# One-core mixer kernel: VectorE instead of GpSimd sums weight quarters; other budgets for side work; two products of a pair change places and banks swap by pairs

## The chip, the cores and the metric

The kernel runs on one core of one Trainium2 chip. The metric is device time in microseconds, median of several runs of the whole program. Before the change it is 978.81 us (three runs, 978.65 to 979.02).

## What is computed

A chain of three blocks over 4 x 576 tokens of 512 features, all in fp32 with every matrix product made of three rounded products (high x high, high x low, low x high):

```python
def reference(q, k, v, omega, moe_*, moe2_*):
    x = random_feature_attention(q, k, v, omega)          # 8 heads of 64, 128 features
    x = x + (relu(x.T @ w_tok1) @ w_tok2).T               # token mixing
    x = x + relu(x @ moe_w_ch1) @ moe_w_ch2               # first channel MLP, 512 -> 1536 -> 512
    u = x + real(fft(fft(x, axis=1), axis=2))             # over tokens, then features
    un = (u - mean(u)) / sqrt(var(u) + 1e-6)
    return u + relu(un @ moe2_w_ch1) @ moe2_w_ch2         # second MLP, 512 -> 2048 -> 512
```

## The kernel before, in words

Weights come in as 64-bit words. `widen` turns each slab on VectorE (seven instructions, L341 to L372) into two fp32 halves and stores them in DRAM tensors `kept`; this and the transform are **side work**.

The stages, in order of time in the profile: attention (to about 204 us), the first MLP in five token blocks (`ch_block`, to about 536 us), the second MLP in two **plain** blocks (`ff_block`, block 0 of 512 tokens to about 651 us, block 1 of 256 tokens to about 704 us), and two **paired** blocks of 768 tokens (`paired_block`, to the end).

One step of `mlp` is: twelve up-products into a bank H (L776), relu on ScalarE (`hh`, L860), `hl` on VectorE (L861), side work, then the twelve down-products of the step before (L898 in the first MLP, L1259 in the second), and in the plain blocks a second helping of side work. TensorE, VectorE and ScalarE each take their instructions strictly in the order in which this Python code emits them.

`Side` hands out side work. `step(budget)` adds to a credit that is capped at SAVED_US and runs items, each with an estimated cost, from a queue `lead` and then from a queue `rest` until the credit is used; `None` in a queue makes it pause for `apart` steps. CH_US, FF_US and S_US are the budgets of a step in the first MLP, the plain blocks and the paired blocks. In `lead` stand the transforms `dft(b)` (the chains even0 to even4 and odd0 to odd3 on VectorE, L957 to L1024 with L978, feeding the TensorE products L1050 to L1061, then L1077 and L1090) and the normalisations `norm(c)` (L1158 to L1186).

`sum_pair(p)` makes, for the paired blocks, four sums and differences of quarters of the weights of a pair of slabs: one 128x1024 addition and four 128x256 ones on GpSimd (L1214 to L1218), a rounding on ScalarE (L1222), a 128x1024 difference on GpSimd (L1226), and a store by SyncE's queue (L421). It runs for pairs 0 to 6 during block 0 and for pair 7 in block 1. GpSimd has no other arithmetic after attention, only DMA issues.

In `paired_block` each pair of slabs takes seven products by Strassen-like sums, six matmuls each (`product`, L1455), into two banks X and Y, with the down-products of the pair before in between (`run`, L1468):

```python
X = P1;   s1 = X;          Y = P6;  u2 = Y + s1       # L1497, L1499
X += P2;  relu of X;       Y = P5;  vv = Y + u2       # L1461, L1507
Y += P3;  held0 = Y + u2;  X = P7;  held1 = X + vv    # L1513, L1515
X += P4;  c21 = X + u2;    relu of c21                # L1521, L1461
```

After each of the four parts comes a step of side work (`pace`). In paired block 0 that is the last transform and `norm(3)`. The operands of P3 lie in `buh`, those of P7 in `bul`; for paired block 0 they are made at its start by `prepare_late`.

Of the kernel before, what the change touches and what calls it, by code (L numbers as in the profile page):

```python
# [14 lines left out]
ALU = mybir.AluOpType  # L15
# [5 lines left out]
B, H, S, D, M = 4, 8, 576, 64, 128  # L21
# [11 lines left out]

SLOT0_US, SLOT1_US, SLOT_US, FIRST_US, SHORT_US, CH_US, FF_US, S_US, SAVED_US = 1.2, 0.45, 1.2, 3.9, 1.2, 4.0, 3.0, 1.5, 4.0


NP = NFF // 2
HALF = 384  # L40
# [3 lines left out]
ROWS = PLAIN + PAIRED  # L44
P1, P2, P4, P6, P3, P7, P5 = 0, 1, 3, 4, 5, 6, 7
# [156 lines left out]
class Side:  # L202
# [5 lines left out]
    def __init__(self):  # L208
        self.lead, self.rest, self.issues = [], [], []
        self.credit = 0.0  # L210
        self.steps = 0
        self.apart, self.waited = 1, 0
        self.defer = DEFER

    def later(self, fn, steps=None):
# [9 lines left out]
    def step(self, budget):  # L225
        self.steps += 1
        while self.issues and self.issues[0][0] <= self.steps:
            self.flush()
        self.credit = min(self.credit + budget, SAVED_US)
        for queue in (self.lead, self.rest):  # L230
            while queue:
                if queue[0] is None:
                    self.waited += 1
                    if self.waited >= self.apart:
                        queue.pop(0)
                        self.waited = 0
                    break
                if queue[0][0] > self.credit:
                    return
                item = queue.pop(0)  # L240
                self.credit -= item[0]
                item[1]()
# [60 lines left out]
def mix_kernel(ctx: ExitStack, tc: tile.TileContext, qt, kt, va, om, w1, w2, wch, wff, t1, t2, out):  # L303
# [97 lines left out]
    whole = set()  # L401
# [44 lines left out]
    def bank(tag):  # L446
        if tag not in pools:
            tag = "A"
        if tag == "A" and spare:

            tag = spare.pop(0)
            spare.append(tag)
        pl, bufs = pools[tag]
        return pl.tile([128, 512], F32, tag=tag, name=tag, bufs=bufs)
# [251 lines left out]
    side = Side()  # L706
# [22 lines left out]
    def turns(n, c):  # L729
        return list(range(n)) if c % 2 == 0 else list(range(n))[::-1]  # L730
# [176 lines left out]
    u = mlp0["u"]  # L907
# [6 lines left out]
    u = u2  # L914
# [278 lines left out]
    def ff_split(c, u, kks):  # L1193
        n = 128 * len(ROWS[c])
        for kk in kks:
            pb = bank("S")
            for t in range(len(ROWS[c])):
                pe.transpose(pb[:, t * 128:t * 128 + 128], uns[c, t][:, kk * 128:kk * 128 + 128], ident)
            act.copy(out=u[0][:, kk, 0:n], in_=pb[:, 0:n])
            dve.tensor_tensor(out=u[1][:, kk, 0:n], in0=pb[:, 0:n], in1=u[0][:, kk, 0:n], op=ALU.subtract)  # L1200

    def ff_prepare(c, u):
        return [lambda: (side.until(lambda: (c, len(ROWS[c]) - 1) in uns, side.lead), ff_split(c, u, (0, 1))),
                lambda: ff_split(c, u, (2, 3))]

    def sum_pair(p):

        k = p % 2  # L1210
        w = mix.get((1, p))
        y = cv.tile([128, 1024], F32, tag=f"cvy{k}", name="cvy")
        v = y.rearrange("p (c n) -> p c n", c=4)
        pool.tensor_tensor(out=v, in0=w[:, :, 0], in1=w[:, :, 1], op=ALU.add)  # L1214
        pool.tensor_tensor(out=v[:, 3], in0=v[:, 2], in1=v[:, 3], op=ALU.add)
        pool.tensor_tensor(out=v[:, 2], in0=v[:, 0], in1=v[:, 2], op=ALU.subtract)
        pool.tensor_tensor(out=v[:, 0], in0=v[:, 3], in1=v[:, 0], op=ALU.subtract)
        pool.tensor_tensor(out=v[:, 1], in0=v[:, 1], in1=v[:, 0], op=ALU.subtract)  # L1218
        so = cv.tile([128, 2, 1024], F32R, tag=f"cvo{k}", name="so")

        def high():
            act.copy(out=so[:, 0], in_=y)  # L1222
            side.later(low, 1)

        def low():
            pool.tensor_tensor(out=so[:, 1], in0=y, in1=so[:, 0], op=ALU.subtract)  # L1226
            side.later(store, 3)

        def store():
            keep(sync, kept[1, p][:, 4:8], so)  # L1230
            whole.add((3, p))

        side.later(high, 4)

    def put_out(r, acc):
        x = row(r)
# [144 lines left out]
    for at_ in range(1, NBLK):  # L1381

        if at_ == 3:
            leave_slots()
            f2 = ctx.enter_context(tc.tile_pool(name="f2", bufs=1, side="right", reuse_waits="tile"))
            l3 = ctx.enter_context(tc.tile_pool(name="l3", bufs=2, side="right", reuse_waits="tile"))
        if at_ == 4:
            side.lead += norm(0)
        if at_ in (3, 4):
            side.lead += dft(at_ - 3)  # L1390
        v = operand()
        last = at_ + 1 == NBLK
        ch_block(at_, BLOCKS[at_], u, ff_prepare(0, v) if last else [lambda: ch_split(BLOCKS[at_ + 1], v)],
                 SHORT_US if at_ == 1 else CH_US)
        u = v

    side.apart = 2
    side.lead += norm(1) + dft(2)
    v = operand()
    ff_block(0, u, ff_prepare(1, v), FF_US)()  # L1400
    side.lead += norm(2) + [None, (0.0, begin_ff)] + prepare_early(0) + prepare_early(1)
# [81 lines left out]
    def paired_block(c, todo, uses, after):  # L1483
# [6 lines left out]
                side.step(S_US)  # L1490

        for p_ in range(NP):
            X, Y = (bank("H")[:, 0:HALF] for _ in range(2))
            h = hbuf[4 * (p_ % 2):4 * (p_ % 2) + 4]
            w = ffw.get((1, p_, 0))
            product(X, w[:, 0], P1, True)
            act.copy(out=s1, in_=X)  # L1497
            product(Y, w[:, 1], P6, True)
            dve.tensor_tensor(out=u2, in0=Y, in1=s1, op=ALU.add)  # L1499
            ffw.used()  # L1500
            pace()
            run(todo, 4)
            w = ffw.get((1, p_, 1))
            product(X, w[:, 0], P2, False)
            relu_parts(h[0:2], X)
            product(Y, w[:, 1], P5, True)
            dve.tensor_tensor(out=vv, in0=Y, in1=u2, op=ALU.add)  # L1507
            pace()
            run(todo, 5)
            ffw.used(1 + uses)  # L1510
            w = ffw.get((1, p_, 2))
            product(Y, w[:, 0], P3, False)
            dve.tensor_tensor(out=held[p_][:, 0], in0=Y, in1=u2, op=ALU.add)  # L1513
            product(X, w[:, 1], P7, True)
            dve.tensor_tensor(out=held[p_][:, 1], in0=X, in1=vv, op=ALU.add)  # L1515
            ffw.used()
            pace()
            run(todo, 4)
            w = ffw.get((1, p_, 3))
            product(X, w[:, 0], P4, False)  # L1520
            dve.tensor_tensor(out=c21, in0=X, in1=u2, op=ALU.add)  # L1521
            relu_parts(h[2:4], c21)
            pace()
            run(todo)
            ffw.used(1 + uses)
            if after:
                after()
            after, uses = None, 1
            if p_ == 0:
                acc = [bank("A") for _ in range(RT)]  # L1530
            for s_ in range(2):
                todo += downs(acc, h[2 * s_:2 * s_ + 2], (2, p_, s_), p_ + s_ == 0, p_ + s_ == NP)
# [62 lines left out]
```

## Time and profile before

| | |
|---|---|
| median of three runs | 978.81 us |
| the profiled execution's own time | 980.43 us |
| its span (first to last instruction) | 978.70 us |
| TensorE busy / VectorE busy / GpSimd busy | 943.6 / 631.0 / 180.7 us |
| mean granted TensorE clock | 0.989 of full speed |

In the profile PE is TensorE's matmuls, PEld its weight loads, DVE VectorE, ACT ScalarE, POOL GpSimd, SPq SyncE's queue. A row of the timeline has the start, the duration of the group of like instructions that begins there, the engine, line, operation, tile written and read, shape, count, and in brackets the idle time just before and what ended it. Matmuls are pipelined and their ends modelled, so distances of starts are the safer measure of TensorE's progress.

### The profile page before, as it was taken

The page shows a single profiled execution, that of the slowest core. Times are in us where ns is not written, and L with a number is a line of the kernel's source. Part 1 is how long each engine was busy: PE and PEld are TensorE (multiplying, and loading weights), DVE is VectorE, ACT ScalarE, POOL GpSimd, SP SyncE. Part 2 cuts the span into 40 slices and gives each one's busy share as a digit, 9 for nine tenths or more (in the row PEclk, how much of TensorE's full clock was granted, in tenths as well). Part 3 has the DMA queues.
Part 4 walks back from the last instruction along what each step waited for, and adds up shares of the span by engine and source line. Part 5 has one row for each costly group of instructions (what it writes and reads, how often), then busy time and mean ns, then how long its engine had stood idle before and what let it go on. Part 6 is the DMA issues. An engine that isn't in the chain of part 4 may idle for free.

```text
span 978.7 us, 14096 instructions
## 1 busy us (share of the span) xinstructions
PE 943.6 (96%) x5362; PEld 835.8 (85%) x5362; DVE 631.0 (64%) x1222; ACT 301.1 (31%) x676; POOL 180.7 (18%) x158
## 2 busy tenths in 40 slices
PE   7999998999999999999999996899999999999998
PEld 7999897988889888888888885788888998899986
DVE  5997989886775777767765366446475466543342
ACT  5976666642212322122211111122221113311121
POOL 3443333321210122000004063640000000000000
PEclk9999999999999999999999997999999999999999
DMA  7764454388898576562446374538756666677764
GB/s 265 234 202 171 146 218 154 139 307 322 314 408 331 188 273 228 203 248 108 172 173 224 120 235 152 172 119 331 290 195 206 219 209 213 221 263 256 249 209 162
DMA packets 68258, 216.48 MB, mean 221 GB/s; under 512 B 5600, under 2 KB 14432, under 8 KB 54240
## 3 DMA queue, kind: packets, MB, share of 16 engines
q1 hardware_dynamic: 60992, 172.40, 50.6%
q0 software_dynamic: 7056, 43.06, 12.0%
q8 instruction: 42, 0.69, 0.3%
q14 instruction: 24, 0.20, 0.1%
q10 hardware_dynamic: 144, 0.13, 0.0%
HBM read 169.30 MB, written 42.47 MB: 216 GB/s over the span
## 4 chain that ended last, share of the span: by engine, by line
PE 83%; DVE 13%; ACT 2%; issue 1%; DMA 0%; DVEq 0%; ACTq 0%
PE H L776 21%; PE A L898 15%; PE A L1468 13%; PE H L1455 11%; PE A L1259 6%; PE A L506 3%; PE N L582 2%; PE A L667 2%; PE H L540 2%; DVE mx L520 1%; PE S L1077 1%; DVE cvo L364 1%; PE S L1090 1%; PE S L680 1%; PE A L565 1%
## 5 line engine op out<-in xcount | busy, mean ns | idle before, releaser
L776 PE MATMUL H<-uh,w 128*128 128x512 f32 (+1 forms) x736 | 214.9, 360 | 1.5 <-ACT x L621 1.5
L776 PEld LDWEIGHTS H<-uh,w 128*128 128x128 f32 x736 | 133.5, 190 | 22.1 <-ACT x L621 1.7
L860 ACT ACTIVATE hh<-H 128x512 fp32r<-128x512 f32 (+1 forms) x92 | 49.1, 533 | 298.2 <-PE H L776 298.1
L776 PE MATMUL H<-ul,w 128*128 128x512 f32 (+1 forms) x368 | 132.0, 359 | 0.0
L861 DVE SCALAR_TENSOR_TENSOR hl<-H,hh 128x512 fp32r<-128x512 f32 (+1 forms) x92 | 56.0, 608 | 107.9 <-ACT hh L860 107.6
L898 PE MATMUL A<-hh,w 128*128 128x512 f32 (+1 forms) x480 | 108.7, 369 | 0.0
L1468 PE MATMUL A<-w2t,b 128*128 128x512 f32 x384 | 100.8, 394 | 0.0
L898 PEld LDWEIGHTS A<-hh,w 128*128 128x128 f32 x480 | 84.2, 188 | 15.0
L1455 PE MATMUL H<-b,w1t 128*128 128x384 f32 x480 | 92.0, 337 | 1.7 <-DVE t L1515 0.9
L1455 PEld LDWEIGHTS H<-b,w1t 128*128 128x128 f32 x480 | 83.9, 188 | 7.3 <-DVE t L1515 3.4
L1468 PEld LDWEIGHTS A<-w2t,b 128*128 128x128 f32 x384 | 70.6, 188 | 11.6
L776 PEld LDWEIGHTS H<-ul,w 128*128 128x128 f32 x368 | 69.8, 190 | 10.0
L524 ACT ACTIVATE f<-A,mx 128x128 f32<-128x128 f32 x200 | 57.6, 393 | 27.6 <-DVE mx L520 23.5
L898 PE MATMUL A<-hl,w 128*128 128x512 f32 (+1 forms) x240 | 59.2, 368 | 0.0
L1259 PE MATMUL A<-w,hh 128*128 128x512 f32 x192 | 52.5, 406 | 0.0
L520 DVE TENSOR_REDUCE mx<-A 128x4 f32<-128x512 f32 x71 | 48.1, 681 | 3.1 <-PE A L506 2.1
L898 PEld LDWEIGHTS A<-hl,w 128*128 128x128 f32 x240 | 42.6, 188 | 7.6
L364 DVE SCALAR_TENSOR_TENSOR cvo<-cvo,stg 128x1024 f32<-128x1024 int32 (+2 forms) x32 | 41.1, 1283 | 0.0
L540 PE MATMUL H<-v,f 128*128 128x65 f32 x320 | 40.1, 270 | 0.9 <-ACT f L524 0.9
L1259 PEld LDWEIGHTS A<-w,hh 128*128 128x128 f32 x192 | 35.3, 194 | 6.2
L540 PEld LDWEIGHTS H<-v,f 128*128 128x128 f32 x320 | 38.9, 191 | 1.3 <-ACT f L524 1.1
L360 DVE SCALAR_TENSOR_TENSOR cvo<-cvy,cvo 128x1024 int32<-128x1024 int32 (+2 forms) x32 | 38.6, 1207 | 0.5
(254 smaller groups left out, 1728.6 us busy)
## 6 DMA issues: line engine op xcount, KB each, us to landing
w<-kept SPq DMA_DIRECT2D x60, 1024.0 KB, 6.7
w2t<-kept SPq DMA_DIRECT2D x55, 512.0 KB, 4.9
w1t<-kept SPq DMA_DIRECT2D x48, 512.0 KB, 4.8
stg<-in_wff_dram POOLq DMA_DIRECT2D x16, 1024.0 KB, 6.3
kept<-cvo POOLq DMA_DIRECT2D x13, 1024.0 KB, 6.2
stg<-in_wch_dram SPq DMA_DIRECT2D x9, 1024.0 KB, 6.0
kept<-cvo POOLq DMA_DIRECT2D x16, 512.0 KB, 7.0
kept<-so SPq DMA_DIRECT2D x16, 512.0 KB, 9.4
```

Of the source, the lines that this page charges most:

```text
L360: dve.scalar_tensor_tensor(out=st["h"], in0=st["y"].bitcast(I32), scalar=-0x80000000, in1=st["h"], op0=ALU.bitwise_and, op1=ALU.bitwise_or)
L364: dve.scalar_tensor_tensor(out=st["l"].bitcast(F32), in0=st["l"], scalar=2.0 ** 32, in1=st["lw"].bitcast(U32), op0=ALU.mult, op1=ALU.add)
L520: dve.tensor_reduce(out=mx, in_=p4, axis=AX.X, op=ALU.max, negate=True)
L524: act.activation(out=f[:, hh], in_=p4[:, hh], func=AF.Exp, bias=mx[:, hh])
L540: pe.matmul(out=kvp[b, g][:, hh * 65:hh * 65 + 65], lhsT=ft["k", i, g][:, hh, :], rhs=src["v", i, int(off > 0)][:, 4 * g + hh, :], start=( ...
L776: pe.matmul(out=hb[:, 0:n], lhsT=w(a, kk), rhs=u[:, kk, 0:n], start=(c == 0), stop=(c == 11))
L860: act.activation(out=hh, in_=hb[:, 0:n], func=AF.Relu)
L861: dve.scalar_tensor_tensor(out=hl, in0=hb[:, 0:n], scalar=0.0, in1=hh, op0=ALU.max, op1=ALU.subtract)
L898: pe.matmul(out=acc[i][:, 0:cols], lhsT=a[:, cs], rhs=v, start=(n == 0 and c_ == 0), stop=(n == NCH - 1 and c_ == 2))
L1259: pe.matmul(out=acc[t], lhsT=a[:, t * 128:t * 128 + 128], rhs=w, start=(n == 0 and c_ == 0), stop=(n == NFF - 1 and c_ == 2))
L1455: pe.matmul(out=to, lhsT=w[:, a, cs], rhs=v[:, q], start=(start and n == 0), stop=(n == 5), skip_group_check=True)
L1468: pe.matmul(out=acc[t], lhsT=h[n // 2][:, t * 128:t * 128 + 128], rhs=w[:, n % 2], start=(begins and n == 0), stop=(ends and n == 2))
```

## The change

- `sum_pair` makes its sums on VectorE instead of GpSimd, in line with the other work of that engine, and earlier after one another: the first addition at once, the other four at the next step, the rounding one step after those, the difference one step later (cost estimates 1.2, 1.5 and 1.2), the store two steps after that.
- Budgets: CH_US 4.0 to 4.3, FF_US 3.0 to 3.8, SAVED_US 4.0 to 4.6.
- `norm(0)` and `norm(1)` go to the queue `rest`, and each queue counts its own pauses.
- In a pair, P7 and its sum come ahead of P3 and its sum, and every second pair takes the two banks in the other order.

```diff
-SLOT0_US, SLOT1_US, SLOT_US, FIRST_US, SHORT_US, CH_US, FF_US, S_US, SAVED_US = 1.2, 0.45, 1.2, 3.9, 1.2, 4.0, 3.0, 1.5, 4.0
+SLOT0_US, SLOT1_US, SLOT_US, FIRST_US, SHORT_US, CH_US, FF_US, S_US, SAVED_US = 1.2, 0.45, 1.2, 3.9, 1.2, 4.3, 3.8, 1.5, 4.6
...
-        for queue in (self.lead, self.rest):
+        for n, queue in enumerate((self.lead, self.rest)):
             while queue:
                 if queue[0] is None:
-                    self.waited += 1
-                    if self.waited >= self.apart:
+                    self.waited[n] += 1
+                    if self.waited[n] >= self.apart:
                         queue.pop(0)
-                        self.waited = 0
+                        self.waited[n] = 0
                     break
...
-        return [lambda: (side.until(lambda: (c, len(ROWS[c]) - 1) in uns, side.lead), ff_split(c, u, (0, 1))),
+        return [lambda: (side.until(lambda: (c, len(ROWS[c]) - 1) in uns, side.rest), ff_split(c, u, (0, 1))),
...
+        side.until(lambda: p not in turns(NP, 0)[2:] or (3, p - 2) in whole, side.lead)
         w = mix.get((1, p))
...
-        pool.tensor_tensor(out=v, in0=w[:, :, 0], in1=w[:, :, 1], op=ALU.add)
-        pool.tensor_tensor(out=v[:, 3], in0=v[:, 2], in1=v[:, 3], op=ALU.add)
-        pool.tensor_tensor(out=v[:, 2], in0=v[:, 0], in1=v[:, 2], op=ALU.subtract)
-        pool.tensor_tensor(out=v[:, 0], in0=v[:, 3], in1=v[:, 0], op=ALU.subtract)
-        pool.tensor_tensor(out=v[:, 1], in0=v[:, 1], in1=v[:, 0], op=ALU.subtract)
         so = cv.tile([128, 2, 1024], F32R, tag=f"cvo{k}", name="so")
+        dve.tensor_tensor(out=v, in0=w[:, :, 0], in1=w[:, :, 1], op=ALU.add)
+        side.credit -= 1.2
+
+        def sums():
+            dve.tensor_tensor(out=v[:, 3], in0=v[:, 2], in1=v[:, 3], op=ALU.add)
+            dve.tensor_tensor(out=v[:, 2], in0=v[:, 0], in1=v[:, 2], op=ALU.subtract)
+            dve.tensor_tensor(out=v[:, 0], in0=v[:, 3], in1=v[:, 0], op=ALU.subtract)
+            dve.tensor_tensor(out=v[:, 1], in0=v[:, 1], in1=v[:, 0], op=ALU.subtract)
+            side.later(high, 1)
 
         def high():
             act.copy(out=so[:, 0], in_=y)
-            side.later(low, 1)
+            side.later(lambda: side.lead.insert(0, (1.2, low)), 1)
 
         def low():
-            pool.tensor_tensor(out=so[:, 1], in0=y, in1=so[:, 0], op=ALU.subtract)
-            side.later(store, 3)
+            dve.tensor_tensor(out=so[:, 1], in0=y, in1=so[:, 0], op=ALU.subtract)
+            side.later(store, 2)
...
-        side.later(high, 4)
+        side.lead.insert(0, (1.5, sums))
...
         if at_ == 4:
-            side.lead += norm(0)
+            side.rest[0:0] = norm(0)
...
-    side.lead += norm(1) + dft(2)
+    side.lead += [(0.0, lambda: side.rest.extend(norm(1)))] + dft(2)
...
-            X, Y = (bank("H")[:, 0:HALF] for _ in range(2))
+            X, Y = [bank("H")[:, 0:HALF] for _ in range(2)][::(1, -1)[p_ % 2]]
...
+            product(X, w[:, 1], P7, True)
+            dve.tensor_tensor(out=held[p_][:, 1], in0=X, in1=vv, op=ALU.add)
             product(Y, w[:, 0], P3, False)
             dve.tensor_tensor(out=held[p_][:, 0], in0=Y, in1=u2, op=ALU.add)
-            product(X, w[:, 1], P7, True)
-            dve.tensor_tensor(out=held[p_][:, 1], in0=X, in1=vv, op=ALU.add)
```

Where the instructions move. The lines of the changed program are higher by 2 from `sum_pair` on and by 5 behind it.

**VectorE in block 0, around the even chain of the third transform.** `cvy` and `so` are the sums, `w` the weights, `fo` and `fv` the transform. Before:

```order
L861 SCALAR_TENSOR_TENSOR hl<-H,hh 128x512
L973 TENSOR_TENSOR fv<-fo 128x289
L974 TENSOR_TENSOR fv<-fo 128x289
L975 COPY fv<-sp 1x578
L984 TENSOR_TENSOR fo<-fv 128x3x144
L985 COPY fo<-fv 128x3
L986 TENSOR_TENSOR fo<-fv 128x3x144
L992 TENSOR_REDUCE al<-fo 128x3
L993 TENSOR_REDUCE al<-fo 128x3
L994 TENSOR_TENSOR fo<-al 128x3
L978 COPY fo<-fo 128x3x99
L861 SCALAR_TENSOR_TENSOR hl<-H,hh 128x512
```

Now:

```order
L1216 TENSOR_TENSOR cvy<-w 128x1024
L861 SCALAR_TENSOR_TENSOR hl<-H,hh 128x512
L1220 TENSOR_TENSOR cvy<-cvy 128x256
L1221 TENSOR_TENSOR cvy<-cvy 128x256
L1222 TENSOR_TENSOR cvy<-cvy 128x256
L1223 TENSOR_TENSOR cvy<-cvy 128x256
L992 TENSOR_REDUCE al<-fo 128x3
L993 TENSOR_REDUCE al<-fo 128x3
L994 TENSOR_TENSOR fo<-al 128x3
L978 COPY fo<-fo 128x3x99
```

L973 to L986 now stand one step earlier than L992 to L978, and the sums fill the places between two `hl`.

**VectorE in paired block 0, second pair, between `u2` and `vv`.** `bul<-H,buh` is the relu's low half. Before:

```order
L968 TENSOR_TENSOR fv<-fv 128x289
L969 TENSOR_TENSOR fo<-fo,fv 128x2x289
L1461 SCALAR_TENSOR_TENSOR bul<-H,buh 128x384
L1507 TENSOR_TENSOR tmp_6646<-H,tmp_6645 128x384
L973 TENSOR_TENSOR fv<-fo 128x289
L974 TENSOR_TENSOR fv<-fo 128x289
L975 COPY fv<-sp 1x578
```

Now:

```order
L968 TENSOR_TENSOR fv<-fv 128x289
L969 TENSOR_TENSOR fo<-fo,fv 128x2x289
L973 TENSOR_TENSOR fv<-fo 128x289
L974 TENSOR_TENSOR fv<-fo 128x289
L975 COPY fv<-sp 1x578
L1466 SCALAR_TENSOR_TENSOR bul<-H,buh 128x384
L1512 TENSOR_TENSOR tmp_6652<-H,tmp_6651 128x384
```

Three more instructions of the transform stand ahead of the relu's low half and of `vv`.

**SyncE's queue from the end of block 0 into block 1.** The L421 rows are the stores of sums of pairs, L735 and L738 the loads of weights for block 1. Before:

```order
L1241 DMA out_dram<-U 128x512 x4
L421 DMA kept_4321<-so 128x4x256 x2
L735 DMA w<-kept_4206 128x2048
L738 DMA w<-kept_4249 128x2048
L421 DMA kept_4755<-so 128x4x256 x2
L735 DMA w<-kept_4060 128x2048
L738 DMA w<-kept_4133 128x2048
L421 DMA kept_5105<-so 128x4x256 x2
```

Now:

```order
L421 DMA kept_4292<-so 128x4x256 x2
L1246 DMA out_dram<-U 128x512 x4
L421 DMA kept_4671<-so 128x4x256 x2
L735 DMA w<-kept_4176 128x2048
L738 DMA w<-kept_4250 128x2048
L421 DMA kept_4870<-so 128x4x256 x2
L735 DMA w<-kept_4060 128x2048
L738 DMA w<-kept_4104 128x2048
```

The stores of pairs 5, 6 and 7 each stand earlier; that of pair 7 is now ahead of the two loads that it followed.

## Rows read from the trace of the kernel before

**Rows 1.** The page, part 1: busy us (share of the span), instructions.
```profile
PE 943.6 (96%) x5362; PEld 835.8 (85%) x5362; DVE 631.0 (64%) x1222; ACT 301.1 (31%) x676; POOL 180.7 (18%) x158
```

**Rows 2.** Waits of TensorE from 204 us on: us in total, times, longest us.
```profile
PE S L1050 <- DVE fo L984: 5.3, 1, 5.3
...
PE H L1455 <- DVE tmp L1507: 1.0, 1, 1.0
```

**Rows 3.** Timeline of TensorE, first stretch in block 0.
```profile
586.23 1.98 PE L1259 MATMUL A<-w,hh 128*128 128x512 f32 x8
...
595.67 0.77 PE L1050 MATMUL S<-t_sb,fo 128*128 128x129 f32 x2 [5.31 <-DVE fo L984]
...
604.08 1.99 PE L1259 MATMUL A<-w,hh 128*128 128x512 f32 x8
```

**Rows 4.** The same timeline, undisturbed work and the second stretch.
```profile
606.82 0.38 PE L1050 MATMUL S<-t_sb,fo 128*100 128x129 f32 x2
...
607.39 0.47 PE L776 MATMUL H<-uh,w 128*128 128x512 f32 x1
...
612.96 0.39 PE L776 MATMUL H<-uh,w 128*128 128x512 f32 x1
...
624.55 0.39 PE L776 MATMUL H<-uh,w 128*128 128x512 f32 x1
```

**Rows 5.** Windows: us, busy (count) of PE, PEld, DVE, ACT, POOL; clock, DMA share, GB/s.
```profile
598.00:600.00 2.00, 2.00 (x10) 2.00 (x11) 0.84 (x2) 0.39 (x1) 0.00 (x0) 0.50 1.00 357
```

**Rows 6.** Timeline of VectorE and GpSimd in the first stretch.
```profile
577.23 2.39 POOL L1226 TENSOR_TENSOR so<-cvy,so 128x1024 fp32r<-128x1024 f32 x1 [5.53 <-ACT so L1222]
577.24 2.40 DVE L1175 TENSOR_TENSOR z<-z,ve 128x2 f32<-128x2 f32 x1
...
590.83 2.44 POOL L1214 TENSOR_TENSOR cvy<-w 128x1024 f32<-128x1024 f32 x1
...
590.99 2.59 DVE L974 TENSOR_TENSOR fv<-fo 128x289 f32<-128x289 f32 x1
```

**Rows 7.** A single line: ns min/median/max, first and last start.
```profile
L974 DVE TENSOR_TENSOR fv<-fo x4: 443/448/2593, 399.8 to 725.6; 128x289 f32<-128x289 f32 x4
```

**Rows 8.** Groups on GpSimd: busy us, mean ns of one, idle before.
```profile
L1226 POOL TENSOR_TENSOR so<-cvy,so 128x1024 fp32r<-128x1024 f32 x8 | 19.8, 2472 | 77.7 <-ACT so L1222 77.7
L1214 POOL TENSOR_TENSOR cvy<-w 128x1024 f32<-128x1024 f32 x8 | 19.2, 2397 | 0.5
...
L1216 POOL TENSOR_TENSOR cvy<-cvy 128x256 f32<-128x256 f32 x8 | 6.3, 789 | 0.6
```

**Rows 9.** Groups on VectorE by shape: busy us, mean ns of one, idle before.
```profile
L861 DVE SCALAR_TENSOR_TENSOR hl<-H,hh 128x512 fp32r<-128x512 f32 x64 | 44.1, 689 | 73.5 <-ACT hh L860 73.3
...
L372 DVE SCALAR_TENSOR_TENSOR cvo<-cvo,cvy 128x1024 fp32r<-128x1024 f32 x28 | 35.7, 1275 | 0.0
...
L1507 DVE TENSOR_TENSOR tmp<-H,tmp 128x384 f32<-128x384 f32 x16 | 8.9, 557 | 1.0 <-PE H L1455 1.0
...
L1186 DVE TENSOR_SCALAR un<-U,mv,y 128x512 f32<-128x512 f32 x16 | 8.6, 598 | 0.1
...
L968 DVE TENSOR_TENSOR fv<-fv 128x289 f32<-128x289 f32 x4 | 1.8, 440 | 0.0
```

**Rows 10.** Timeline of TensorE at the start of paired block 0.
```profile
716.76 3.41 PE L1455 MATMUL H<-b,w1t 128*128 128x384 f32 x18 [0.87 <-DVE t L1515]
...
725.32 1.31 PE L1455 MATMUL H<-buh,w1t 128*128 128x384 f32 x6 [0.98 <-DVE tmp L1507]
...
749.34 1.34 PE L1455 MATMUL H<-b,w1t 128*128 128x384 f32 x6 [0.87 <-DVE tmp L1499]
```

**Rows 11.** Timeline of SyncE's queue around block 1.
```profile
651.43 2.23 SPq L1241 DMA_DIRECT2D out_dram<-U  x4
...
665.84 0.50 SPq L735 DMA_DIRECT2D w<-kept  x1
...
669.44 1.13 SPq L421 DMA_DIRECT2D kept<-so  x2
```

More of the change, by code (lines that the diff above doesn't have):

```diff
@@ L211, in __init__ @@
         self.steps = 0
-        self.apart, self.waited = 1, 0
+        self.apart, self.waited = 1, [0, 0]
         self.defer = DEFER
```

## The prediction

> **What bounds the kernel now.** I read the page first: TensorE is busy 96% of the span [rows 1], so only time in which it waits, or runs at the lower clock, can be won. Then the list of what TensorE waits for. Behind 204 us it is almost always VectorE: the longest wait, 5.3 us, is for the transform's chain, and there are waits of about 1 us in the paired block [rows 2]. Third, the timeline of TensorE at these waits, by distances of starts.
>
> Block 0 has two stretches. In the first, twelve down-products start at 586.23, then twelve transform matmuls and twelve up-products should follow, and the next down-products start only at 604.08: 17.85 us [rows 3]. Undisturbed, twelve products take 606.82 - 604.08 = 2.74 us and six transform matmuls 607.39 - 606.82 = 0.57 us [rows 3, 4]. So 2 x 2.74 + 2 x 0.57 = 6.62 us were due, and 11.2 us are lost. In the second stretch, from 612.96 to 624.55, twelve up-products, eight transform matmuls and twelve down-products took 11.59 us [rows 4]; due are 2 x 2.74 + 8 x 0.095 = 6.24, lost 5.35. Together **16.6 us**. Part of it is clock: behind the long wait the granted clock is 0.50, that is 1.2 GHz, while TensorE is busy again [rows 5].
>
> Last, what VectorE does there. A product of 128x2 numbers takes 2.40 us, and it begins with a GpSimd difference of 2.39 us; L974 takes 2.59 us beside a GpSimd addition of 2.44 us [rows 6]. The same L974 has a median of 0.45 us elsewhere [rows 7]. So VectorE's instructions with SBUF operands stand still while GpSimd's sums run, VectorE falls behind by these excesses, and TensorE waits for the transform and then for its clock.
>
> **The change, part by part.**
>
> *GpSimd's sums go.* With them goes what holds VectorE up, and with that the 16.6 us, if nothing takes their place. The waits did not come from VectorE's amount of work, so the question is whether the added work leaves cover.
>
> *VectorE's sums come.* No row shows them. The nearest are a 128x1024 instruction with two SBUF operands, 1.28 us, and a 128x289 one, 0.44 us [rows 9]: 2 x 1.28 + 4 x 0.44 = 4.3 us for a pair, which I take. From below, with a quarter of 1.28 us for each 128x256 operation, it would be 2 x 1.28 + 4 x 0.32 = 3.8 us; from above, at GpSimd's own rate, 2.47 + 2.40 + 4 x 0.79 = 8.0 us [rows 8]. I take 4.3, from the rows nearest in size and engine, and keep 8.0 for a rival. The Trainium skill ("GPSIMD Engine Reference", When to use GPSIMD) gives a price of its own, GpSimd about twice as slow as VectorE with two inputs: half of 8.0, an estimate of 4.0 us, by which the count below has 59 us instead of 61 and the sum is the same; no run here shows it yet.
>
> Is there cover? I counted the order of the changed program over thirteen steps of block 0 (from the second half of the transform's even chain on). VectorE has thirteen `hl` at 0.69 = 9.0 us [rows 9], transform and normalisation about 23 us at undisturbed durations like the 0.44 and 0.45 of [rows 7, 9], and seven first additions, seven sets of quarters and six differences, 7 x (1.28 + 1.76) + 6 x 1.28 = 29 us: 61 us. TensorE has 13 x 5.48 = 71 us of products and some 6 us of transform matmuls: 77 us. The heaviest single step (end of the even chain, a difference, a first addition) has about 6.8 us of VectorE against 6.0 of TensorE, and the next one 5.0. `hl` may come late by down-, up- and two thirds of down-products, 7.3 us less its own 1.3, before TensorE waits; a lag of 0.8 us is covered. Were the cover gone, each us of VectorE would be a us of TensorE. I set the new waits in block 0 to 0, with a loss of up to 3 us (the lag of 0.8 us and two misplaced operations of 1.28) kept for the range.
>
> *Budgets and queues.* One group of the transform's second stage moves from block 0 into the first MLP, and one from block 1 into block 0. TensorE does the same matmuls in any place; what hides them is that VectorE's steps in the first MLP come to at most 5.6 us (even0 to even2 with `hl`) against 5.5 of TensorE, with the same 6 us of allowed lag. Cost 0; uncovered, a few tenths. Block 1 likewise: SyncE's queue there is a rival below.
>
> *P7 before P3, banks by pairs.* Away from paired block 0's transform TensorE does not wait in these loops, so only the waits of 0.87, 0.98 and 0.87 us count [rows 10]. (a) First pair: P4 no longer waits behind two sums, but P7 now needs the second half of `bul`, which `prepare_late` finishes last: gain 0.2. (b) Second pair: P7 no longer waits for `vv`, 0.56 us [rows 9], but because the credit holds 4.6 instead of 4.0, L973 to L975 (3 x 0.45 us [rows 7]) now stand ahead of the relu: 0.98 - 0.56 + 1.35 = 1.77, loss 0.8. (c) Third pair: odd chain now ahead of `c21` instead of `u2`, and the bank swap gives P6 a whole product more: about 0.55 for 0.87, gain 0.3. (d) Eighth pair: `norm(3)`'s end and six `un` at 0.60 us [rows 9] now stand ahead of `c21`, whose relu the last down-products need: about 4.2 us against 3.6 of cover, loss 0.6. Net loss 0.9 us; bounds: a gain of 2.7 (all three waits go, none comes) and a loss of 4 (b and d each 1.5 worse).
>
> **Sum.** -16.6 + 0 + 0 + 0.9 = -15.7 us. The profiled execution took 980.43 us (span 978.70); it should become 964.7. It stands 1.62 above the median of the runs, so the median of 978.81 becomes **963.1 us**. About 0.2%, 2 us, can be told from no change.
>
> **The rivals.**
>
> *All paired waits go too:* 978.8 - 16.6 - 2.7 = 959.5. For it: the reordering gives each wait at least half a us. Against: the larger credit bundles the side work there. Chance 0.08.
>
> *VectorE becomes the bound in block 0*, at GpSimd's price of 8.0 us a pair: 7 x (2.40 + 3.16) + 6 x 2.47 = 54 us of sums instead of 29, VectorE 86 against TensorE's 77, a loss of 9: 972. For it only that no row has these sums; against it the 1.28 us row. The Trainium skill ("Perfetto Trace Analysis", Optimizing Scalar/DVE Operations) advises the opposite move, work from VectorE to GpSimd, where VectorE is saturated, and adds that it might not help because the two share a read port. By the first half this change would lose; the trace has VectorE at 64% [rows 1], and rows 6 show the second half. Chance 0.07.
>
> *GpSimd is not what holds VectorE up*, or the waits only move: the 16.6 us stay, with the paired loss about 979.7, within the bound. Against: equal instructions of 0.45 and 2.59 us. Chance 0.03.
>
> *Slower: SyncE's queue in block 1.* Pair 7's store now waits for VectorE's difference and stands ahead of eight of the ten weight loads of block 1 (the order of SyncE's queue, above). Before, it was issued at 669.44, 18 us after the outputs at 651.43, and the loads that it now precedes began at 665.84, 14.4 us after [rows 11]. By VectorE's order I put the store at about 13 us, which delays nothing. It decides from about 18 us on: then each us late is a us in which TensorE has no weights, and as in block 0, where about 10 us of waiting cost 16.6, 1.7 with the clock. At 30 us it would cost 20: 983. For that VectorE would have to be 17 us late in a block in which it has 2.7 us of work a step against 2.8. Chance 0.04.
>
> **Numbers.** The forecast has 0.76, with its own range 960 to 968. With the 3 us kept for block 0 and the bounds of the paired block, the range is 959 to 969; it leaves out the last three rivals and what I have not seen (0.02). Faster by more than 0.2%: forecast, first two rivals and half of the unseen, 0.92; the same 0.03; slower 0.05.
>
> **What would show it.** Right: no POOL arithmetic behind attention; L973, L974, L1022, L1175 at 0.17 to 0.46 us everywhere; no TensorE wait over 1 us and clock 1.00 from 545 us to the end of block 0, which is some 16 us shorter; sums at about 1.2 and 0.4 us; a wait of 1.5 to 2 us at the second pair's P7. Wrong: block 0 with VectorE busy throughout and `hl` ending TensorE's waits; waits for weights in block 1; or a wait in the first MLP that was not there.

## The result, and the profile after

The changed kernel takes **964.65 us** (median of four runs, 964.43 to 965.21), the kernel before beside it 978.91 us. The ratio is 0.9852, its 95% interval 0.9835 to 0.9869: 14.3 us less, or 1.5%. The forecast was 963.1 us in a range of 959 to 969; the time lies in the range, 1.5 us above the forecast.

Four views of the profile after answer to those shown of before. The page, part 1, beside [rows 1]:

```profile
PE 937.9 (98%) x5362; PEld 832.7 (87%) x5362; DVE 645.4 (67%) x1270; ACT 302.2 (31%) x676; POOL 117.9 (12%) x110
```

VectorE has 14 us more work, GpSimd 63 us less, and TensorE is busy 98% of the span. The waits of TensorE from 202 us on (us in total, times, longest us), beside [rows 2]:

```profile
PE H L1460 <- DVE bul L1466: 1.9, 1, 1.9
PE H L776 <- ACT x L621: 1.5, 1, 1.5
PE S L1303 <- DVE buh L1298: 1.2, 1, 1.2
PE H L1460 <- ACT bul L1297: 0.9, 1, 0.9
PE H L1460 <- DVE bul L1298: 0.7, 1, 0.7
...
PE A L1473 <- ACT b L1465: 0.3, 1, 0.3
PE S L1090 <- DVE gath L1125: 0.2, 1, 0.2
```

The 5.3 us behind the transform are gone. All the large waits behind the attention's end are now in paired block 0 (L1460, L1303). The windows of block 0 (columns as in [rows 5]):

```profile
570.00:600.00 30.00, 30.00 (x141) 24.97 (x140) 21.63 (x46) 7.22 (x12) 0.00 (x0) 1.00 0.88 282
600.00:625.00 25.00, 25.00 (x125) 21.20 (x124) 16.76 (x33) 5.43 (x9) 0.00 (x0) 1.00 0.63 213
```

TensorE is busy throughout and the granted clock is 1.00, where it was 0.50 in [rows 5]. VectorE has 38 us of work in these 55 us, and GpSimd none. The new sums on VectorE in 550 to 650 us (busy us, mean ns of one, idle before), and below them L974, which stood still in [rows 6]:

```profile
L1231 DVE TENSOR_TENSOR so<-cvy,so 128x1024 fp32r<-128x1024 f32 x8 | 9.8, 1219 | 1.0 <-ACT so L1227 1.0
L1216 DVE TENSOR_TENSOR cvy<-w 128x1024 f32<-128x1024 f32 x8 | 9.7, 1214 | 0.0
...
L1223 DVE TENSOR_TENSOR cvy<-cvy 128x256 f32<-128x256 f32 x8 | 3.4, 426 | 0.3
```
```profile
L974 DVE TENSOR_TENSOR fv<-fo x4: 453/454/455, 397.4 to 707.3; 128x289 f32<-128x289 f32 x4
```

A pair's sums cost 1.22 + 1.21 + 4 x 0.42 = 4.1 us (4.3 was forecast), and all four L974 take 0.45 us. L973, L1022 and L1175 are also at 0.16 to 0.46 us wherever they stand.

Where the time went, by two starts on TensorE: the first product of the MLP and the first P1 of paired block 0. Before, and then after:

```profile
204.73 0.47 PE L776 MATMUL H<-uh,w 128*128 128x512 f32 x1 [1.49 <-ACT x L621]
...
704.42 2.27 PE L1455 MATMUL H<-b,w1t 128*128 128x384 f32 x12
```
```profile
202.81 0.47 PE L776 MATMUL H<-uh,w 128*128 128x512 f32 x1 [1.49 <-ACT x L621]
...
685.56 2.27 PE L1460 MATMUL H<-b,w1t 128*128 128x384 f32 x12
```

| stretch (profiled execution) | before, us | after, us | difference | forecast |
|---|---|---|---|---|
| to the first product | 204.73 | 202.81 | -1.92 | 0 |
| MLP, blocks 0 and 1 | 499.69 | 482.75 | -16.94 | -16.6 |
| paired blocks, to the span's end | 274.28 | 276.24 | +1.96 | +0.9 |
| outside the span | 1.73 | 2.80 | +1.07 | 0 |
| own time | 980.43 | 964.60 | -15.83 | -15.7 |

The second row is block 0's gain net of transform matmuls that changed places, as the prediction had it: up to the first down-product of block 0 TensorE takes 4.6 us more, in block 0 18.9 us less, and in block 1 2.6 us less. The sum is met almost to the tenth, but partly by accident: the first row hides that the third and the fourth came out worse. The experiments below settle what the second row rests on, and what the third.

### The profile page after: what moved, and what is told of

Same layout as the page of the kernel before. It is cut to its first block, busy times and chain, and to the rows that moved or that the text cites. A ratio compares the mean times of both kernels' runs of the same rounds, so it can differ in the third digit from the quotient of the medians.

```text
span 961.8 us, 14086 instructions
## 1 busy us (share of the span) xinstructions
PE 937.9 (98%) x5362; PEld 832.7 (87%) x5362; DVE 645.4 (67%) x1270; ACT 302.2 (31%) x676; POOL 117.9 (12%) x110
## 3 DMA queue, kind: packets, MB, share of 16 engines
q0 software_dynamic: 7056, 43.06, 12.2%
## 4 chain that ended last, share of the span: by engine, by line
PE 87%; DVE 11%; ACT 1%; issue 1%; DMA 0%; DVEq 0%; ACTq 0%
PE H L776 22%; PE A L898 15%; PE A L1473 13%; PE H L1460 12%; PE A L1264 7%; PE A L506 3%; PE H L540 2%; PE A L667 2%; DVE mx L520 2%; PE N L582 2%; PE S L1077 1%; DVE cvo L364 1%; DVE x L598 1%; PE S L1090 1%; PE S L680 1%
## 5 line engine op out<-in xcount | busy, mean ns | idle before, releaser
L1460 PE MATMUL H<-b,w1t 128*128 128x384 f32 x480 | 92.9, 339 | 0.0
L1460 PEld LDWEIGHTS H<-b,w1t 128*128 128x128 f32 x480 | 86.2, 190 | 4.2 <-DVE tmp L1526 0.3
L1473 PEld LDWEIGHTS A<-w2t,b 128*128 128x128 f32 x384 | 70.6, 188 | 12.2 <-ACT b L1465 0.7
L1264 PE MATMUL A<-w,hh 128*128 128x512 f32 x192 | 50.5, 395 | 0.0
L1465 ACT ACTIVATE b<-tmp 128x384 fp32r<-128x384 f32 x16 | 8.4, 525 | 106.9 <-DVE tmp L1526 106.9
```

What stands on the lines that cost most here:

```text
L1264: pe.matmul(out=acc[t], lhsT=a[:, t * 128:t * 128 + 128], rhs=w, start=(n == 0 and c_ == 0), stop=(n == NFF - 1 and c_ == 2))
L1460: pe.matmul(out=to, lhsT=w[:, a, cs], rhs=v[:, q], start=(start and n == 0), stop=(n == 5), skip_group_check=True)
L1473: pe.matmul(out=acc[t], lhsT=h[n // 2][:, t * 128:t * 128 + 128], rhs=w[:, n % 2], start=(begins and n == 0), stop=(ends and n == 2))
```

## The experiments

Lines of a variant built from the changed kernel can be a few higher than in the changed kernel itself.

### Engine or order: undo one, do one alone

**The sums back on GpSimd**, everything else as changed:

```diff
-        dve.tensor_tensor(out=v, in0=w[:, :, 0], in1=w[:, :, 1], op=ALU.add)
+        pool.tensor_tensor(out=v, in0=w[:, :, 0], in1=w[:, :, 1], op=ALU.add)
```
(and so the other five)

> The changed kernel with one thing undone: the six sums of sum_pair are GpSimd instructions again; budgets, queues, pairs of products and banks stay as changed. Theory T (GpSimd's sums held VectorE's instructions back): VectorE instructions of 0.45 to 0.7 us that meet a GpSimd sum last 2.0 to 2.6 us again, TensorE waits in block 0 again, and the time goes up by at least 8 us, to 972 to 980 us (976 as a middle). Rival R (the new budgets and queues brought the gain, by starting the transforms earlier): it stays at 964 to 966 us although GpSimd is busy again.

Measured: 963.79 us, ratio 0.9851 (0.9824 to 0.9877). Theory T is wrong in this form: with GpSimd busy again nothing is lost. The only wait of TensorE from 540 us to the paired blocks is the 0.2 us that the changed kernel has too. But VectorE's instructions still stand still. Its timeline in block 0, GpSimd's and TensorE's:

```profile
577.99 0.81 DVE L1003 TENSOR_TENSOR fo<-x 128x576 f32<-128x576 f32 x1
...
584.19 2.38 DVE L1017 COPY fv<-sp 1x288 f32<-1x288 f32 x1
586.61 2.54 DVE L1022 TENSOR_TENSOR fo<-fv 128x286 f32<-128x286 f32 x1
```
```profile
583.72 2.69 POOL L1231 TENSOR_TENSOR so<-cvy,so 128x1024 fp32r<-128x1024 f32 x1 [3.12 <-ACT so L1227]
586.37 2.46 POOL L1216 TENSOR_TENSOR cvy<-w 128x1024 f32<-128x1024 f32 x1
```
```profile
592.72 0.38 PE L1060 MATMUL S<-t_sb,fo 128*128 128x129 f32 x2
```

L1022 takes 2.54 us instead of 0.45, beside a GpSimd addition. What is new is the room: from L1003, the first instruction of the transform's odd chain, to the matmul that reads the chain's end (L1060) there are 592.72 - 577.99 = 14.7 us. Before, there were 617.71 - 608.54 = 9.2, 1.87 of them a wait of TensorE. Some 4 us of standing still fit into the one and not into the other.

The odd chain is the smaller of the two losses, 5.35 us. The even chain, behind which 11.2 us were lost, has moved out of GpSimd's way. It starts at 548.02; GpSimd has then been idle for a while, and its next sum begins when only the last instructions of the chain are left. L974, which took 2.59 us in [rows 6], takes 0.45 again (VectorE, then GpSimd):

```profile
554.34 0.45 DVE L974 TENSOR_TENSOR fv<-fo 128x289 f32<-128x289 f32 x1
```
```profile
559.79 2.39 POOL L1231 TENSOR_TENSOR so<-cvy,so 128x1024 fp32r<-128x1024 f32 x1 [39.39 <-ACT so L1227]
```

**The engine alone**: the kernel before, with its six sums on VectorE and its old order, budgets and queues:

```diff
-        pool.tensor_tensor(out=v, in0=w[:, :, 0], in1=w[:, :, 1], op=ALU.add)
+        dve.tensor_tensor(out=v, in0=w[:, :, 0], in1=w[:, :, 1], op=ALU.add)
```
(and so the other five)

> The kernel before with one thing done: the six sums are VectorE instructions; budgets, queues, pairs of products and banks stay old. Theory T: most of block 0's loss goes, 14 to 16 us less, 963 to 966 us, with the paired blocks as before (first pair at full clock). Rival R: without the larger budgets VectorE's queue is not emptied in time and the gain does not come, 975 us or more; in between (967 to 974) both would have a share.

Measured: 964.53 us, ratio 0.9846 (0.9832 to 0.9861). So the engine alone is also worth the whole gain. The odd chain has only 604.23 - 597.09 = 7.1 us here, and without GpSimd that is enough; one wait of 1.2 us is left in block 0 (L1051 for L978).

**The budgets alone**, with GpSimd's sums:

```diff
-CH_US, FF_US, S_US, SAVED_US = 4.0, 3.0, 1.5, 4.0
+CH_US, FF_US, S_US, SAVED_US = 4.3, 3.8, 1.5, 4.6
```
(the last four of the row of numbers)

> The kernel before with one thing done: the five numbers of the change (4.3, 3.8 and 4.6 for 4.0, 3.0 and 4.0); GpSimd still makes the sums, in the old order, and all queues are old. Theory Q (with GpSimd's sums kept, what helped was that the transform's even steps were put ahead of the normalisation, so that they ran at 547 to 562 us instead of 584 to 598 us): the transform stays behind the normalisation, beside the sums, most of the waits of block 0 stay, 974 to 980 us. Theory B (larger budgets give the steps enough room): 964 to 968 us.

Measured: 979.33 us, ratio 0.9995 (0.9978 to 1.0012). Nothing, as theory Q said. TensorE now reaches L1050 at 593.92 - 9.31 = 584.61, 2.4 us behind the even chain's first instruction (582.19); before it came 6.4 us behind it (595.67 - 5.31 - 583.98). So the wait grows, while the odd chain's two waits go:

```profile
593.92 0.77 PE L1050 MATMUL S<-t_sb,fo 128*128 128x129 f32 x2 [9.31 <-DVE fo L984]
```

**The queues alone**, with GpSimd's sums:

```diff
-            side.lead += norm(0)
+            side.rest[0:0] = norm(0)
...
-    side.lead += norm(1) + dft(2)
+    side.lead += [(0.0, lambda: side.rest.extend(norm(1)))] + dft(2)
```
(and each queue counts its own pauses)

> The kernel before with one thing done: the queues of the change (the normalisations of blocks 0 and 1 go to the rest queue, each queue counts its own steps); GpSimd still makes the sums, in the old order, under the old budgets. Theory Q: the transform's even steps run before most of the sums and its odd steps have a step more between them, so TensorE's waits in block 0 (11.2 and 5.35 us lost) go but for 1 to 3 us: 964 to 967 us. Theory B (the budgets, or the new steps inside sum_pair, are what helped): 972 us or more.

Measured: 974.43 us, ratio 0.9951 (0.9931 to 0.9970), 4.5 us: theory B by its number, with a part of what theory Q said. The even chain has moved ahead of the sums and TensorE no longer waits for L984; the odd chain has not got room (a wait of 3.2 us for L1022). Another 3.8 us of waits stand in block 1, and the next run shows where they come from.

**Queues and budgets together** (the two edits above), `sum_pair` as before:

> The kernel before with the change's queues and budgets together; sum_pair stays wholly as before (GpSimd, five sums at a time, the difference in a pass outside the credits), and so do the paired blocks. Theory P (queues and budgets need each other: the one puts the transform's even steps ahead of the sums, the other gives its odd steps the credit to stay ahead): 963 to 967 us, like the changed kernel with its sums on GpSimd. Theory S (what was still missing is sum_pair's own new order, its four sums a step of their own and its difference paid from the credits): 970 to 976 us, like the queues alone.

Measured: 974.94 us, ratio 0.9946 (0.9926 to 0.9967). Theory S: what was missing is `sum_pair`'s new order of steps. Its VectorE and TensorE, at the same place as above:

```profile
568.48 0.75 DVE L1003 TENSOR_TENSOR fo<-x 128x576 f32<-128x576 f32 x1
...
569.93 2.53 DVE L1010 TENSOR_TENSOR sp<-fv 1x288 f32<-1x288 f32 x1
...
576.25 0.43 DVE L1022 TENSOR_TENSOR fo<-fv 128x286 f32<-128x286 f32 x1
```
```profile
576.84 0.46 PE L1060 MATMUL S<-t_sb,fo 128*128 128x129 f32 x2 [1.06 <-DVE fo L1022]
```

From L1003 to L1060 it has 8.4 us, 1.06 of them a wait, against 14.7 with the sums' new steps, and GpSimd does the sums in both. From the first product to P1 it takes 695.46 - 203.04 = 492.4 us, against 686.53 - 203.81 = 482.7 there. What differs ahead of the paired blocks is `sum_pair`, and the waits show two ways in which it counts. Of TensorE's 6.7 us of waits from 540 us to P1, 2.7 are for the odd chain and its next product. In the changed kernel each sum draws 1.2 to 1.5 us from the credit that also pays the transform, whose steps so come further apart; that these draws make the room is read from the code. The other 4.0 us are in block 1, with a granted clock of 0.50 behind them (664 to 666 us), and the longest of them comes from a store of the sums. ScalarE prepares operands of the paired blocks in the memory of `so`; it stands 8.27 us until the store has landed, and the relu behind it comes late (ScalarE, then TensorE):

```profile
663.30 0.51 ACT L1292 CAST b<-tmp 128x384 fp32r<-128x384 f32 x1 [8.27 <-DMA kept<-so]
```
```profile
664.15 2.07 PE L1259 MATMUL A<-w,hh 128*128 128x512 f32 x4 [2.38 <-ACT hh L860]
```

The queues alone have the same wait, 8.03 us on ScalarE; the changed kernel, and its variant with the sums on GpSimd, have none for a store there. So the earlier store has a share in the gain too. Neither the draws nor the store were tried alone.

### Does GpSimd hold VectorE up by itself?

**Additions that nobody reads**, on the changed kernel:

```diff
+        z = so.bitcast(F32)
+        pool.memset(z[:, 0], 0.0)
+        for _ in range(3):
+            pool.tensor_tensor(out=z[:, 1], in0=z[:, 0], in1=z[:, 0], op=ALU.add)
```

> The changed kernel, and in each of the eight calls of sum_pair GpSimd gets one memset and three additions of 128x1024 with two SBUF inputs, on memory that is overwritten later; no sum depends on them, nothing else is moved. Theory T (a GpSimd addition with two inputs keeps VectorE waiting by itself, without anyone needing its result): some 7 us of GpSimd work per pair, VectorE instructions beside it last up to about 2.4 us, waits of TensorE in block 0 return, 968 to 980 us. Rival (in the kernel before what cost was the late result of GpSimd, not its presence): 964 to 966 us.

**Memsets in their place**, eight of `z[:, 1]` for the three additions:

> As the run with GpSimd additions, but GpSimd gets nine memsets of 128x1024 per pair, which write and do not read. Theory T (what holds VectorE back is GpSimd's reading): VectorE's instructions keep their length, 964 to 966 us. Rival (any GpSimd work on SBUF holds VectorE back): as with the additions, in proportion to GpSimd's busy time, 967 us or more.

Measured: with the additions 980.45 us, ratio 1.0009 (0.9995 to 1.0023), so 15.8 us more than the changed kernel and the whole gain gone; with the memsets 965.62 us, ratio 0.9856 (0.9841 to 0.9872). VectorE, GpSimd and TensorE in the first, one pair:

```profile
637.78 2.00 DVE L1224 TENSOR_TENSOR cvy<-cvy 128x256 f32<-128x256 f32 x1
639.81 2.00 DVE L1225 TENSOR_TENSOR cvy<-cvy 128x256 f32<-128x256 f32 x1
641.85 2.00 DVE L1226 TENSOR_TENSOR cvy<-cvy 128x256 f32<-128x256 f32 x1
643.88 0.42 DVE L1227 TENSOR_TENSOR cvy<-cvy 128x256 f32<-128x256 f32 x1
```
```profile
637.22 6.34 POOL L1220 TENSOR_TENSOR so<-so 128x1024 f32<-128x1024 f32 x3
```
```profile
644.96 0.44 PE L1198 MATMUL S<-ident,un 128*128 128x128 f32 x2 [3.34 <-DVE U L1091]
```

Each of three instructions of 0.42 us takes 2.00 us beside one addition, and the fourth, behind the last addition, takes 0.42 again. TensorE waits 3.34 us for L1091, which stands behind them on VectorE. With the memsets nothing of that is seen, though GpSimd works longer for a pair, 9 x 0.96 = 8.6 us against 0.95 + 6.34 = 7.3 (groups of 540 to 660 us, GpSimd, and of 550 to 650 us, VectorE):

```profile
L1220 POOL MEMSET so<- 128x1024 f32 x48 | 45.9, 956 | 2.4
```
```profile
L1224 DVE TENSOR_TENSOR cvy<-cvy 128x256 f32<-128x256 f32 x8 | 3.3, 418 | 0.1
```

The expectation was not right in one thing: the sums do not read GpSimd's results, but ACT's rounding writes to the same memory and must wait for it. In the memset run VectorE's difference waited 9.1 us in all for GpSimd that way, and TensorE 1.0 us behind it. In the run with the additions the path costs more. ScalarE, then TensorE:

```profile
618.11 1.04 ACT L1231 CAST so<-cvy 128x1024 fp32r<-128x1024 f32 x1 [10.68 <-POOL so L1220]
```
```profile
619.49 0.74 PE L1090 MATMUL S<-ident,x 128*128 128x128 f32 x4 [2.69 <-ACT e L1101]
```

A second wait of 2.41 us follows, for L1085 on VectorE behind the late difference. So of TensorE's 11.0 us of waits from 570 to 655 us, 5.1 come from the order in this memory; the rest, the 3.34 us above among them, are for other work of VectorE. The 15.8 us, and the 14.8 between the two runs, so measure more than the standing still, and the run with the additions does not rule out its rival, a late result of GpSimd. For the kernel before, its own trace does: in the first stretch, from 576.24 to 598.42 us, VectorE waits for nothing, and its instructions only take longer.

The Trainium skill ("SBUF — State Buffer", Who interferes with whom) says that a VectorE instruction with two SBUF inputs contends with a GpSimd instruction that reads SBUF and not with one that only writes. Both rows agree: 2.00 us beside additions, 0.42 us beside memsets.

### The paired block

**The old order of P3 and P7** and of the banks, everything else as changed:

```diff
-            X, Y = [bank("H")[:, 0:HALF] for _ in range(2)][::(1, -1)[p_ % 2]]
+            X, Y = (bank("H")[:, 0:HALF] for _ in range(2))
...
-            product(X, w[:, 1], P7, True)
-            dve.tensor_tensor(out=held[p_][:, 1], in0=X, in1=vv, op=ALU.add)
             product(Y, w[:, 0], P3, False)
             dve.tensor_tensor(out=held[p_][:, 0], in0=Y, in1=u2, op=ALU.add)
+            product(X, w[:, 1], P7, True)
+            dve.tensor_tensor(out=held[p_][:, 1], in0=X, in1=vv, op=ALU.add)
```

> The changed kernel with P3 before P7 again and the banks no longer swapped in odd pairs. Theory A (the paired part's miss comes from the new order: in the first pair P7 waits twice for bul, 0.86 and 0.67 us, and the clock falls behind it): P3 needs buh, ready about 0.9 us earlier, the two waits shrink to about 0.2, the clock stays at 1.00 in 696 to 702 us, and 0.5 to 1.8 us are gained: 963 to 964 us. Theory B (the new order pays as forecast in the later pairs, 0.3 to 0.6 us, and the clock's fall is chance): 965 to 965.5 us.

Measured: 965.42 us, ratio 0.9860 (0.9847 to 0.9874). Theory B by the sign, but 0.8 us is within the 2 us that can be told. What theory A said of the first pair came true: the two waits for `bul` are gone, and the clock stays at 1.00 there. But the second pair's wait is larger, 2.33 us, now for `vv`, and the clock falls to 0.50 behind that one (710 to 712 us):

```profile
708.45 1.77 PE L1460 MATMUL H<-buh,w1t 128*128 128x384 f32 x6 [2.33 <-DVE tmp L1512]
```

**The cap of 4.0 back from the paired blocks on**:

```diff
+    side.saved = 4.0
     carry = prepare_late(0) + prepare_late(1), 0, None
```

> The changed kernel with the cap on saved credit back at 4.0 from the paired blocks on, so that the three transform instructions of lines 973 to 975 stand behind the second pair's relu and its vv on VectorE instead of ahead of them. Theory A: the second pair's wait for bul, 1.86 us, falls by about 1.35 to 0.5 us: 963 to 964 us. Theory B: the displaced instructions make a later pair or the transform wait as long: 964.5 to 965.5 us.

Measured: 962.75 us, ratio 0.9835 (0.9821 to 0.9848). Theory A: the second pair's wait is 0.52 us instead of 1.86, though the transform's matmuls then wait 0.74. From P1 to the span's end it takes 960.9 - 687.64 = 273.3 us, 3.0 less than the changed kernel's 276.24. About 1.3 of that is the wait and the rest is clock, which the cap is not shown to change (the run with the sums on GpSimd has the larger cap and a clock of 1.00 too):

```profile
697.30 0.44 PE L1461 MATMUL H<-bul,w1t 128*128 128x384 f32 x1 [0.86 <-ACT bul L1298]
698.41 0.62 PE L1461 MATMUL H<-bul,w1t 128*128 128x384 f32 x2 [0.67 <-DVE bul L1299]
...
699.91 3.28 PE L1461 MATMUL H<-b,w1t 128*128 128x384 f32 x18
...
707.87 1.31 PE L1461 MATMUL H<-bul,w1t 128*128 128x384 f32 x6 [0.52 <-DVE bul L1467]
...
713.15 0.49 PE L1052 MATMUL S<-t_sb,fo 128*128 128x129 f32 x2 [0.74 <-DVE fo L979]
```

Its first rows are the control for the clock. The changed kernel's first pair has the same waits, and then its clock falls:

```profile
695.23 0.44 PE L1460 MATMUL H<-bul,w1t 128*128 128x384 f32 x1 [0.86 <-ACT bul L1297]
696.34 0.62 PE L1460 MATMUL H<-bul,w1t 128*128 128x384 f32 x2 [0.67 <-DVE bul L1298]
...
698.31 4.42 PE L1460 MATMUL H<-b,w1t 128*128 128x384 f32 x18
...
708.75 1.33 PE L1460 MATMUL H<-bul,w1t 128*128 128x384 f32 x6 [1.86 <-DVE bul L1466]
```
```profile
696.00:698.00 2.00, 1.66 (x8) 1.67 (x9) 1.40 (x3) 0.36 (x1) 0.00 (x0) 0.82 0.15 59
698.00:700.00 2.00, 2.00 (x8) 2.00 (x8) 0.56 (x1) 0.00 (x0) 0.00 (x0) 0.50 0.04 11
700.00:702.00 2.00, 2.00 (x11) 2.00 (x10) 0.94 (x2) 0.83 (x2) 0.00 (x0) 0.83 0.82 281
```

Eighteen products take 4.42 us against 3.28. With the cap back, and in the run with the sums on GpSimd, the clock is 1.00 there.

**P7's parts made early** in `prepare_late`:

```diff
             dve.tensor_tensor(out=xb, in0=pb, in1=xb, op=ALU.subtract)
+            parts_of(P7, q, xb)
             parts_of(P3, q, pb)
...
-            parts_of(P7, q, xb)
             parts_of(P4, q, xa)
```

> The changed kernel with prepare_late making P7's parts in its second step, right after xb, ahead of P3's parts. Theory A: bul is ready about 0.95 us earlier, the first pair's two waits (0.86 and 0.67) shrink to about 0.6 together; if that is enough for the clock to stay at 1.00 another 1.0 us is gained: 962.7 to 963.9 us. Theory B: P3's parts, now later, cost it back (buh also frees a bank that transposes wait for, 1.24 us now): 964.5 to 965.5 us.

Measured: 965.40 us, ratio 0.9856 (0.9841 to 0.9870). Theory B: the two waits for `bul` fall from 1.53 to 0.63 us, but the wait for `buh` grows from 1.24 to 1.74, a wait of 0.86 for L1518 comes behind, and the clock falls here too: twelve products at 692.16 take 3.90 us.

**The six steps of `prepare_late` by twos** behind P1, P6 and P2, with P7's parts early:

```diff
             act.copy(out=s1, in_=X)
+            if p_ == c == 0:
+                run(todo, 2)
...
-            run(todo, 4)
+            run(todo, 2 if p_ == c == 0 else 4)
...
             relu_parts(h[0:2], X)
+            if p_ == c == 0:
+                run(todo, 2)
```

> As the run with P7's parts early, and the six steps of prepare_late spread over the first pair by twos, behind P1, P6 and P2, instead of four behind P6 and two behind P5. Theory A: transposes and products alternate, so the waits of the first pair (0.28, 1.24, 0.86, 0.67 us) go but for some 0.5 us, and the clock stays at 1.00: 3 to 3.5 us less, 961 to 962 us. Theory B: the transposes still wait for their two banks behind VectorE and ACT, and at least half of the waits stays: 963 to 964.5 us.

Measured: 964.22 us, ratio 0.9850 (0.9836 to 0.9863). Theory B: of four waits two are left (1.21 and 0.15 us), and a new one takes their place, since `vv` now stands on VectorE behind more parts and P3's bank waits for it:

```profile
698.35 1.34 PE L1460 MATMUL H<-buh,w1t 128*128 128x384 f32 x6 [1.92 <-DVE tmp L1516]
```

**The cap and the spread together** (the three edits above):

> The changed kernel with the cap of 4.0 from the paired blocks on, P7's parts made early, and prepare_late spread over the first pair by twos. If what the cap gave (1.9 us against the changed kernel) and what the spread gave (0.4) add up: 962 to 962.6 us. If the spread's new wait for vv (1.92 us behind P7 in the first pair) takes as much as it gives: 962.5 to 963.5 us.

Measured: 962.36 us, ratio 0.9819 (0.9790 to 0.9848). It is level with the cap alone, and the two expectations cannot be told apart; the wait for `vv` is there again (1.9 us). Both lie about 2 us below the changed kernel, which is the bound of what can be told; the interval of the cap alone overlaps the changed kernel's own. The cap's gain is the one that a wait in the trace accounts for.

## Why the prediction was right, and where it was wrong

**Block 0, -16.6 us: the size was right.** From the first product to the first P1 the time falls by 16.94 us, TensorE's waits in block 0 are gone and the clock is 1.00. The two lost stretches, read with their clock, were the right thing to add up.

**What it was put down to: half right.** "With them goes what holds VectorE up" is shown: the engine alone gives 14.5 us, and GpSimd additions that nobody reads stretch VectorE's instructions again (a part of the 15.8 us that they cost). But the step **"Budgets and queues. ... Cost 0"** failed as a statement of what these parts do. With the sums left on GpSimd, queues, budgets and the new steps of `sum_pair` give 15.2 us by themselves. Each half of the change removes the loss, so together they give no more than either. The prediction asked what the moves cost and not what they would gain if the sums stayed. It saw the even chain move one step apart, and counted neither that the chain would run ahead of GpSimd's sums nor the distance from a chain's first instruction to the matmul that reads it. The rival "GpSimd is not what holds VectorE up" is wrong by L1022's 2.54 us; what it had hold of is that the waits also go when GpSimd keeps the sums, because the chains have moved ahead or have room.

**VectorE's sums: right.** 4.1 us a pair against 4.3; the bound of 8.0, and the rival that VectorE becomes the bound, are out: 38 us of its work in 55. In the memset run even waits of 9.1 us in all on VectorE, the longest 5.5, cost TensorE only 1.0. The estimate from the Trainium skill ("GPSIMD Engine Reference", When to use GPSIMD), 4.0 us, was a little nearer.

**SyncE's queue: right.** The store of pair 7 is issued 12.2 us after the outputs (about 13 was forecast), and no wait of TensorE in block 1 follows:

```profile
635.15 2.23 SPq L1246 DMA_DIRECT2D out_dram<-U  x4
...
647.35 2.24 SPq L421 DMA_DIRECT2D kept<-so  x2
```

**The paired block, +0.9 us: mis-sized, it measured +1.96.** In two runs with the new pairs, the larger cap and a clock of 1.00 there, the stretch takes 274.6 us (sums on GpSimd: 961.1 - 686.53; memsets: 963.0 - 688.36), only 0.3 above the 274.28 of before. So at full clock the net loss is 0.3 us, and the fall of the clock behind the first pair's waits, which the prediction did not have, adds about 1.7. Term by term: (a) from P1 to P4 it takes 12.2 us in those runs against 12.34 before, gain 0.1 (0.2 forecast); in the changed kernel itself 12.75, and its next eighteen products take 1.1 us more than 3.28, both by the clock. (b) a wait of 1.86 us, 1.77 forecast; its cause is confirmed, since the old cap brings it to 0.52. (c) the third pair's wait is gone, gain 0.9 (0.3). (d) 0.3 us (0.6).

**The base.** The prediction set the sum against a profiled execution that stood 1.62 us above the median, and took those 1.6 us as an offset that stays. They were a stretch of low clock in the attention, 0.93 in 150 to 200 us, which the profile after does not have (1.00). Two runs built from the kernel before, the engine alone and the budgets alone, reach the first product at 202.63 and 202.93 us, like the changed kernel. So -1.92 us there belongs to that execution and not to the change, and it hides that the paired blocks and the time outside the span came out 2.1 us worse than forecast.

**Open.** The time outside the span is 1.73 us in the profile before, and 2.8 to 3.2 in the four runs of the changed kernel. In the runs built from the kernel before it is 1.8 to 1.9, whichever part of the change they carry; in those built from the changed kernel 1.7 to 3.3. No run here isolates which part lengthens it.

## What to carry to other kernels

Where two engines hold each other up, ask two things of the chain that TensorE waits for. Can it run ahead of the other engine's work? And how far is its first instruction from the matmul that reads its end? An instruction that stands still costs only what that distance does not hold. A row that waits for a late result is another matter than one that takes longer; the bracket behind it tells which. When a change does two things, price each as if the other were left out; two cures for one loss do not add up. And read the clock of the profiled execution in every stage before it is made the base of a sum.

## What was not expected

- **The same waits, another clock.** The first pair's waits of 0.86 and 0.67 us are equal within 0.01 us in four runs; behind them the clock falls to 0.50 (1.2 GHz) in the changed kernel and stays at 1.00 in three others (sums on GpSimd, memsets, the old cap). What decides is not visible in the rows and was not isolated; the fall is worth about 1.7 us.
- **Memsets leave additions alone.** 46 us of GpSimd memsets beside VectorE leave its 128x256 additions at 0.42 us; three additions in the same place bring them to 2.00. A copy of VectorE's is stretched a little: L1017 takes 0.68 us beside memsets and 0.30 in the changed kernel.
- **More credit, longer wait.** Larger budgets alone leave the time as it was and make the longest wait 9.31 us instead of 5.31.
